# One even product for each pair of rows, and mirror rows stored by index

## The chip, the cores and the metric

The kernel runs on one core of a Trainium2 chip. The time is the device time of one execution, in microseconds (us). It was run three times, and once more under the hardware profiler, on the same kind of core; the profile times each instruction of that execution.

## The reference

The input x has 8 images of 3072 rows and 256 columns. The reference takes a two-dimensional Fourier transform of each image, keeps the real part, and puts the 24576 resulting rows through a small feed-forward layer with three inputs to a maximum:

```python
X = np.fft.fft(np.fft.fft(x, axis=1), axis=2).real
h = np.maximum(np.maximum(x @ w1, x @ w2), x @ w3)   # x: the 24576 rows of X
out = h @ w_out                                      # 256 -> 768 -> 256
```

All of x, the weights (256 x 768 and 768 x 256) and the output are float32.

## The kernel before

**The mathematics.** A row of the transform at sequence position s and its mirror at 3072 - s have the same even part and opposite odd parts, up to a sign in one column. The kernel therefore holds for each image two bf16 tiles, `tE` (even) and `tO` (odd), each 128 by 1536, one column for each pair of rows, and gets from each pair the row and the mirror row. Row 1536 of each image is made apart (`l2_mid`).

The maximum is written as a linear part plus a rest: w1's part goes straight through w_out (folded together in the weight `gw`: columns 0 to 255 for the even part, 256 to 511 for the odd one; `gwr` is the odd half with the sign of the mirror). The rest needs the maximum of 0 and two differences, whose weights are `gE`, `gO` and, for the step from the row to its mirror, `gD`.

**The stages.** For each image:

- Stage 1 (`Mix.s`, L305): 64 small matmuls of 96 columns in 13 pieces, each evicted by ScalarE (ACT) to `ub`.
- Folds (`Mix.fold`, L316): VectorE (DVE) adds and subtracts mirrored parts into `zE` and `zO`.
- Stage 2 (`Mix.k`, L337): six groups of 128-column matmuls, each evicted by ACT into 512 columns of `tE` or `tO`. `Mix.end` (L365) makes the middle row's column and lets GpSimd (POOL) write reversed copies `tEr` and `tOr` (L374, L375).
- Hidden layer: 18 *units* for each image, three blocks of 512 columns by six slices `jc` of 128 hidden features. A unit does four matmuls of 512 columns (L384, L385) into two PSUM banks, `pse2` and `pse3`. ACT then takes the relu of the first (L398), and DVE the maximum with the second (L399) into `hp`. One unit later `finish` adds the two `gD` matmuls (L392) on the same banks, and ACT and DVE make `hm`, the mirror's hidden values, in the same way; the last argument `hm[:, jc, ::-1]` writes them in reversed order.
- Output layer (`l2_block`, L411): for each of four sub-blocks of 128 columns, and for the row and its mirror, eight matmuls of 256 columns into one half of a PSUM bank `po`: even part (L402), odd part (L404), six hidden slices (L407). Then DVE copies `po` to `ot` (L427) and the SyncE queue (SP) issues the stores (L434): two of 128 rows, or, for the sub-block with rows 0 and 12, four shorter ones. A store writes every 24th row of the output, 1 KB each. The reversed copies are what make the mirror's rows come out in that order.

**What sets the order.** The order is written out by hand; each engine works through its own instructions in that order, and waits on semaphores. In each unit the code issues: the four matmuls of this unit and its `hp` operations; `finish` of the unit before; up to 11 matmuls of the output layer of the block before (`l2_some(11)`, a generator that is advanced one matmul at a time); and then what `plan` holds for this unit (L536 to L555): stage-1 pieces, folds and stage-2 groups of the next image, the weight products of the start, the casts of the image after the next (`turn_chunk`, POOL, L117), and the loads (`fetch`, SP). A block has 64 output matmuls and six units, so 66 turns.

PSUM has eight banks: two for `pse2`, two for `pse3`, two for `po`, and two (`ps_f`) that stage 1, stage 2 and the weight products share in turn. `ot` has four buffers.

**Start and end.** x for image 0 comes through POOL's queue (converted on the way) and SP's; stage 1 of image 0 needs all of it. The tables of sines are made meanwhile. At the very end the output layer of the last block runs by itself.

Of the kernel before, what the change touches and what calls it, by code (L numbers as in the profile page):

```python
# [11 lines left out]
INT32 = mybir.dt.int32  # L12
# [21 lines left out]
def kernel(  # L34
# [48 lines left out]
    gE = [consts.tile([128, DFF], BF16, name=f"gE{i}", tag=f"gE{i}") for i in range(2)]  # L83
    gO = [consts.tile([128, DFF], BF16, name=f"gO{i}", tag=f"gO{i}") for i in range(2)]
    gD = [consts.tile([128, DFF], BF16, name=f"gD{i}", tag=f"gD{i}") for i in range(2)]
    gw = consts.tile([128, 512], BF16, tag="gw")
    gwr = consts.tile([128, 256], BF16, tag="gwr")
    sgn = consts.tile([128, 1], FP32, tag="sgn")
    dif = consts.tile([128, 1], FP32, tag="dif")
    t_mid = consts.tile([128, 2, B], BF16, tag="t_mid")  # L90
# [68 lines left out]
    for jh in range(2):  # L159
# [4 lines left out]
        if jh == 0:  # L164
            first_half = wld
    nc.gpsimd.dma_start(out=wout_bf.rearrange("p (jc c) -> p jc c", jc=NJC),
                        in_=moe_w_out.rearrange("(jc p) c -> p jc c", jc=NJC))
    nc.gpsimd.memset(zO.rearrange("p (c r) -> p c r", r=26)[:, :, 24:26], 0.0)
    nc.gpsimd.memset(zO[:, 0:26], 0.0)

# [100 lines left out]
    def prep_second():  # L271

        for jp in range(NJC // 2):
            pst = ps_f.tile([128, 512], FP32, name="pst", tag="ps")
            for k in range(2):
                jc = jp * 2 + k
                for fc in range(2):
                    nc.tensor.matmul(
                        pst[:, k * 256:(k + 1) * 256],
                        w1_bf[:, fc * DFF + jc * 128: fc * DFF + jc * 128 + 128],  # L280
                        md[fc], start=(fc == 0), stop=(fc == 1))
            nc.vector.tensor_copy(out=g1t[:, jp * 512:(jp + 1) * 512], in_=pst)
            yield
        psw = ps_f.tile([128, 512], FP32, name="psw", tag="ps")
        for half in range(2):
            for jc in range(NJC):
                nc.tensor.matmul(
                    psw[:, half * 256:(half + 1) * 256],
                    g1t[:, jc * 256 + half * 128: jc * 256 + half * 128 + 128],
                    wout_bf[:, jc * 256:(jc + 1) * 256],  # L290
                    start=(jc == 0), stop=(jc == NJC - 1))
        nc.vector.tensor_copy(out=gw, in_=psw)
        nc.scalar.activation(out=gwr, in_=psw[:, 256:512], func=AX.Copy, scale=sgn)
        yield

    class Mix:
# [67 lines left out]
        def end(self):  # L364
            er = self.zE.rearrange("p (c r) -> p c r", r=24)  # L365
            orr = zO.rearrange("p (c r) -> p c r", r=26)
            ps3 = ps_f.tile([128, 512], FP32, name="ps3", tag="ps")
            nc.tensor.matmul(ps3[:, 0:1], er[:, :, 0], cos_t[:, 64:65], start=True, stop=True)
            nc.tensor.matmul(ps3[:, 1:2], orr[:, :, 0], nsin_t[:, 64:65], start=True, stop=False)
            nc.tensor.matmul(ps3[:, 1:2], orr[:, :, 24], cos_t[:, 64:65], start=False, stop=True)  # L370
            nc.scalar.copy(out=t_mid[:, :, self.b], in_=ps3[:, 0:2])
            tEr = t_pool.tile([128, NHALF], BF16, name="tEr", tag="tEr")
            tOr = t_pool.tile([128, NHALF], BF16, name="tOr", tag="tOr")
            nc.gpsimd.tensor_copy(tEr, self.tE[:, ::-1])  # L374
            nc.gpsimd.tensor_copy(tOr, self.tO[:, ::-1])  # L375
            self.flipped = tEr, tOr

    def unit_plus(te, to, jc, n):

# [18 lines left out]
        nc.scalar.activation(out=stmp[:, 0:n], in_=pses[0][:, 0:n], func=AX.Relu)  # L398
        nc.vector.tensor_tensor(out=dst, in0=src3, in1=stmp[:, 0:n], op=ALU.max)  # L399

    def l2_half(po, te, to, wo, hcols, n):
        nc.tensor.matmul(po, te, gw[:, 0:256], start=True, stop=False)  # L402
        yield
        nc.tensor.matmul(po, to, wo, start=False, stop=False)  # L404
        yield
        for jc in range(NJC):
            nc.tensor.matmul(po, hcols(jc), wout_bf[:, jc * 256:(jc + 1) * 256],  # L407
                             start=False, stop=(jc == NJC - 1))
            yield

    def l2_block(b, blk, hp, hm, tt):  # L411

        base = b * S
        for sub in range(4):
            slot = blk * 4 + sub
            r = slot + 1
            po = ps_o.tile([128, 512], FP32, name="po", tag="po")
            cp = slice(slot * 128, slot * 128 + 128)
            cm = slice((11 - slot) * 128, (12 - slot) * 128)
            sp = slice(sub * 128, sub * 128 + 128)  # L420
            sm = slice((3 - sub) * 128, (4 - sub) * 128)
            yield from l2_half(po[:, 0:256], tt[0][0][:, cp], tt[0][1][:, cp],
                               gw[:, 256:512], lambda jc: hp[:, jc, sp], 128)
            yield from l2_half(po[:, 256:512], tt[1][0][:, cm], tt[1][1][:, cm],
                               gwr, lambda jc: hm[:, jc, sm], 128)
            ot = out_pool.tile([128, 512], FP32, name="ot", tag="ot")
            nc.vector.tensor_copy(out=ot, in_=po)  # L427
            if r <= 11:
                stores = [(0, 128, base + r, 0), (0, 128, base + 24 - r, 256)]
            else:  # L430
                stores = [(0, 64, base, 0), (64, 128, base + 12, 0),
                          (0, 64, base + 1548, 256), (64, 127, base + 1560, 256)]
            for (p0, p1, row, c) in stores:
                nc.sync.dma_start(out=out[row: row + 24 * (p1 - p0 - 1) + 1: 24, :],  # L434
                                  in_=ot[p0:p1, c:c + 256])

    def l2_mid():

        hmid = h_pool.tile([128, NJC, B], BF16, name="hmid", tag="hmid")
        n = NJC * B  # L440
        psm = ps_f.tile([128, 512], FP32, name="psm", tag="ps")
        for i in range(2):
            for jc in range(NJC):
                js = slice(jc * 128, (jc + 1) * 128)
                cs = slice(i * n + jc * B, i * n + (jc + 1) * B)
                nc.tensor.matmul(psm[:, cs], gE[i][:, js], t_mid[:, 0, :],
                                 start=True, stop=False)
# [10 lines left out]
        yield from l2_half(po[0:B, 0:256], t_mid[:, 0, :], t_mid[:, 1, :], gw[:, 256:512],  # L458
                           lambda jc: hmid[:, jc, :], B)
# [6 lines left out]
    def l2_some(n):  # L466
        while n > 0 and l2_queue:
            try:
# [2 lines left out]
            except StopIteration:  # L471
                l2_queue.pop(0)

    m = Mix(0)
    x0f = x0_first.rearrange("p (bb dl) -> p dl bb", dl=64)
    for k in range(13):
        m.s(k, x0f, pool=ps_s if k % 4 else ps_f)
    m.fold(0, 0)
    m.fold(0, 1)
    m.fold(1, 0)  # L480
# [53 lines left out]
                second.pop(0)  # L534

    for (u, fn) in ((0, prep_some), (0, prep_some), (1, prep_some), (1, prep_some),  # L536
                    (2, lambda: m.k(0, 1)), (2, lambda: m.k(1, 1)),
                    (3, prep_some), (3, lambda: m.k(0, 2)), (4, prep_some),
                    (4, lambda: m.k(1, 2)), (4, m.end), (5, prep_some), (5, prep_some),
                    (0, lambda: turn_chunk(1, 0)), (2, lambda: turn_chunk(1, 1)),  # L540
                    (4, lambda: turn_chunk(1, 2)), (6, lambda: turn_chunk(1, 3))):
        at(0, u, fn)
# [2 lines left out]
    for b in range(B - 1):  # L545
# [3 lines left out]
        if b + 2 < B:  # L549
            folds = begin[b] + 8  # L550
            for ch in range(4):
                at(b, folds + (0, 0, 0, 4)[ch], lambda b=b, ch=ch: turn_chunk(
                    b + 2, ch, mix(b + 1).folded))
                if b + 3 < B:
                    at(b, UNITS + (0, 1, 4, 5)[ch], lambda b=b, ch=ch: fetch(b + 3, ch))  # L555

    for b in range(B):
        mm = mixes[b]
# [3 lines left out]
        def finish(prev):  # L562
            pses, to, jc, hm = prev
            unit_minus(pses, to, jc)
            unit_out(pses, hm[:, jc, ::-1], TOKB)

        for blk in range(3):
            cs = slice(blk * TOKB, (blk + 1) * TOKB)
# [2 lines left out]
            for jc in range(NJC):  # L571
# [2 lines left out]
                if prev is not None:  # L574
                    finish(prev)
                prev = (pses, tO[:, cs], jc, hm)
                l2_some(11)
                if b == B - 1 and blk == 0:
                    if jc == 0:
                        middle = l2_mid()  # L580
# [4 lines left out]
            l2_some(1000)  # L585
            if blk == 2:
                finish(prev)
            l2_queue.append((lambda b, blk, hp, hm, mm: l2_block(
                b, blk, hp, hm, ((mm.tE, mm.tO), mm.flipped)))(b, blk, hp, hm, mm))

    l2_some(1000)

# [28 lines left out]
```

## Time and profile before

| what | us |
| --- | --- |
| median of three runs (451.18 to 453.09) | 452.06 |
| the profiled execution | 451.85 |
| its span, first to last instruction | 450.1 |
| first stage-1 matmul starts | 21.62 |
| last copy of `po` starts | 444.30 |
| one relu (L398), mean | 0.604 |
| one cast of x (L117), mean | 3.80 |
| one reversed copy (L374), mean | 1.48 |
| a stage-1 eviction of 480 columns (L314), mean | 0.569 |

The profile's page gives the busy time of each engine, the chain of work that ended last (followed back from the last instruction, each step to what released it), and groups of instructions with their count, total and mean time and the idle time before them. A matmul's mean time there is longer than the distance between two of them, because they overlap in the array: 256 columns show 273 ns, and start about 0.11 us apart. The distance between starts, read in the timeline, is what one costs when PE is full. The waits view lists which operation waited for which, with the total, the number and the longest. In the timeline a row with "xN" merges N equal instructions that follow each other; its duration is that of all.

### The profile page before, as it was taken

To read this page: it belongs to the slowest core of one execution; us is meant where nothing else is said; L and a number is where in the kernel's file an instruction comes from. 1 tells how busy PE (TensorE), PEld (TensorE's weight loads), DVE (VectorE), ACT (ScalarE), POOL (GpSimd) and SP (SyncE) were. 2 spreads that over 40 slices of the span, in tenths; PEclk is the share of its full clock that TensorE was granted. 3 is DMA by queue.
4 is the path that set the end of the run, shared out by engine and by line. 5 is a ranking of instruction groups with operands and counts; after the bars stand their busy time and mean duration, and the time that the engine had idled before them with its cause. 6 is when DMAs were issued, how large, how long until landed. Compare 5 with 4: busy or idle time off the path is not lost.

```text
span 450.1 us, 9342 instructions
## 1 busy us (share of the span) xinstructions
PE 416.6 (93%) x3365; PEld 294.9 (66%) x3424; DVE 306.5 (68%) x640; ACT 253.0 (56%) x472; POOL 144.1 (32%) x77
## 2 busy tenths in 40 slices
PE   0099899999999999999999999999999999999994
PEld 0075577777777677767676677767776677766674
DVE  7645669666876588566966678576966678567672
ACT  3587466556655665556655665556655665545440
POOL 7505810590059002930078002920087000200000
PEclk9999999999999999999999999999999999999998
DMA  9999999498617992198717982299512212112223
GB/s 113 122 162 127 130 153 153 149 160 149 139 49 140 157 172 81 55 152 169 157 47 128 173 156 98 71 160 166 132 48 71 70 57 84 51 47 73 72 80 107
DMA packets 132862, 51.54 MB, mean 115 GB/s; under 512 B 105936, under 2 KB 132816, under 8 KB 132816
## 3 DMA queue, kind: packets, MB, share of 16 engines
q1 hardware_dynamic: 118384, 47.99, 54.6%
q0 software_dynamic: 12848, 2.57, 8.1%
q10 hardware_dynamic: 1584, 0.39, 0.6%
q8 instruction: 26, 0.43, 0.4%
q14 instruction: 20, 0.16, 0.1%
HBM read 28.31 MB, written 25.17 MB: 119 GB/s over the span
## 4 chain that ended last, share of the span: by engine, by line
PE 91%; DMA 4%; issue 1%; ACT 1%; POOL 1%; DVE 1%; POOLq 0%; ACTq 0%
PE po L407 28%; PE pse L384 16%; PE pse L392 14%; PE pse L385 11%; PE ps L312 6%; PE po L402 5%; PE po L404 5%; DMA x<-in_x_dram 3%; PE ps L359 1%; PE ps L357 1%; PE ps L350 1%; PE psg L259 1%; PE ps L353 1%; DMA w_bf<-in_moe_w_dram 1%; POOL x L99 1%
## 5 line engine op out<-in xcount | busy, mean ns | idle before, releaser
L398 ACT ACTIVATE stmp<-pse 128x512 bf16<-128x512 f32 x288 | 167.1, 604 | 72.3 <-PE pse L385 53.4
L399 DVE TENSOR_TENSOR hp<-pse,stmp 128x512 bf16<-128x512 f32 x144 | 99.5, 691 | 116.3 <-ACT stmp L398 74.7
L117 POOL CAST x<-xs 96x2048 bf16<-96x2048 f32 x28 | 105.7, 3803 | 197.7 <-PE pse L392 180.7
L384 PE MATMUL pse<-tE,gE 128*128 128x512 bf16 x287 | 108.9, 379 | 2.8 <-DVE hm L399 0.2
L399 DVE TENSOR_TENSOR hm<-pse,stmp 128x512 bf16<-128x512 f32 x144 | 98.7, 686 | 8.1 <-ACT stmp L398 7.8
L385 PE MATMUL pse<-tO,gO 128*128 128x512 bf16 x234 | 88.6, 379 | 0.5 <-ACT tO L362 0.5
L407 PE MATMUL po<-wout_bf,hp 128*128 128x256 bf16 x576 | 86.1, 273 | 0.1
L407 PE MATMUL po<-wout_bf,hm 128*128 128x256 bf16 x576 | 86.1, 273 | 0.0
L392 PE MATMUL pse<-tO,gD 128*128 128x512 bf16 x284 | 84.8, 379 | 0.3
L314 ACT CAST ub<-ps 128x480 bf16<-128x480 f32 (+1 forms) x104 | 52.2, 563 | 43.8 <-PE ps L312 43.8
L427 DVE COPY ot<-po 128x512 f32<-128x512 f32 x96 | 65.6, 683 | 3.8 <-PE po L407 3.8
L407 PEld LDWEIGHTS <-hp 128*128 128x128 bf16 x576 | 56.4, 98 | 16.3
L407 PEld LDWEIGHTS <-hm 128*128 128x128 bf16 x576 | 56.4, 98 | 16.3
L312 PE MATMUL ps<-m24blk,x 96*128 96x96 bf16 x512 | 33.0, 216 | 21.6 <-DMA w_bf<-in_moe_w_dram 21.6
L392 PEld LDWEIGHTS <-gD 128*128 128x128 bf16 x288 | 27.9, 98 | 32.1
L312 PEld LDWEIGHTS <-x 96*128 96x128 bf16 x512 | 30.3, 112 | 22.7 <-DVE dif L243 21.6
L384 PEld LDWEIGHTS <-gE 128*128 128x128 bf16 x288 | 28.6, 99 | 19.8 <-issue 1.2
L385 PEld LDWEIGHTS <-gO 128*128 128x128 bf16 x288 | 28.2, 98 | 19.1 <-issue 0.8
L362 ACT CAST tO<-ps 128x512 bf16<-128x512 f32 x24 | 14.1, 586 | 29.1 <-PE ps L359 29.1
L402 PE MATMUL po<-gw,tE 128*128 128x256 bf16 x96 | 26.2, 273 | 0.2
L404 PE MATMUL po<-gw,tO 128*128 128x256 bf16 x96 | 26.2, 273 | 0.0
L402 PE MATMUL po<-gw,tEr 128*128 128x256 bf16 x96 | 26.2, 273 | 0.0
(109 smaller groups left out, 356.5 us busy)
## 6 DMA issues: line engine op xcount, KB each, us to landing
out_dram<-ot SPq DMA_DIRECT2D x176, 128.0 KB
xs<-in_x_dram SPq DMA_DIRECT2D x112, 192.0 KB
out_dram<-ot SPq DMA_DIRECT2D x24, 64.0 KB
w_bf<-in_moe_w_dram POOLq DMA_DIRECT2D x6, 192.0 KB, 4.9
xs<-in_x_dram SPq DMA_DIRECT2D x8, 96.0 KB
x<-in_x_dram POOLq DMA_DIRECT2D x8, 96.0 KB, 11.9
out_dram<-ot SPq DMA_DIRECT2D x8, 63.0 KB
xs<-in_x_dram ACTq DMA_DIRECT2D x4, 96.0 KB
```

Of the source, the lines that this page charges most:

```text
L117: cast = nc.gpsimd.tensor_copy(turned[b][:, :, ch * 32:(ch + 1) * 32], raw.pop((b, ch)).rearrange("p (bb dl) -> p dl bb", dl=64))
L312: nc.tensor.matmul(ps1[:, i * 96:(i + 1) * 96], x0[:, d0 + i, :], m24blk, start=True, stop=True)
L314: evict(out=self.ub[:, d0 * 96:d1 * 96], in_=ps1[:, 0:(d1 - d0) * 96])
L384: nc.tensor.matmul(pse[:, 0:n], gE[i][:, js], te, start=True, stop=False)
L385: nc.tensor.matmul(pse[:, 0:n], gO[i][:, js], to, start=False, stop=True)
L392: nc.tensor.matmul(pse, gD[i][:, js], to, start=False, stop=True, skip_group_check=True)
L398: nc.scalar.activation(out=stmp[:, 0:n], in_=pses[0][:, 0:n], func=AX.Relu)
L399: nc.vector.tensor_tensor(out=dst, in0=src3, in1=stmp[:, 0:n], op=ALU.max)
L402: nc.tensor.matmul(po, te, gw[:, 0:256], start=True, stop=False)
L404: nc.tensor.matmul(po, to, wo, start=False, stop=False)
L407: nc.tensor.matmul(po, hcols(jc), wout_bf[:, jc * 256:(jc + 1) * 256], start=False, stop=(jc == NJC - 1))
L427: nc.vector.tensor_copy(out=ot, in_=po)
```

## The change

The output layer is made differently, and some things at the start and the end are moved:

- The even part's product is the same for a row and its mirror. It is now made once, for two sub-blocks at a time, into a bank of `ps_f` named `pl` (two matmuls of 256 columns). ACT copies it to a float32 tile `even`.
- The odd part's products for row and mirror become one matmul of 512 columns over `gw[:, 256:768]`, in which `gwr` is now the last third.
- The mirror's hidden matmuls come first in a sub-block, then the row's. DVE adds `even` to both halves of `po` while it takes them to `ot`.
- `hm`, `tE` and `tO` are read in direct order. The reversed copies are gone. The mirror rows therefore come in falling order and are stored by an indirect DMA of POOL, which takes the row numbers from a table `rows_m` made at the start.
- A sub-block has 15 turns of the generator (the 512-column matmul counts as two), a block 60, and `l2_some` takes 10 a unit.
- The last block goes through its sub-blocks in the order 2, 3, 0, 1, and its last addition is split in two halves.
- At the start eight matmuls on `cos_t` into a bank that nothing reads go ahead of stage 1, and DVE takes two of image 0's 13 evictions. In image 0 the third group of stage 2 moves from units 3 and 4 to 6 and 7, and the weight products are spread one to a unit. Casts and loads of later images are spread over more units.

```diff
-            tEr = t_pool.tile([128, NHALF], BF16, name="tEr", tag="tEr")
-            tOr = t_pool.tile([128, NHALF], BF16, name="tOr", tag="tOr")
-            nc.gpsimd.tensor_copy(tEr, self.tE[:, ::-1])
-            nc.gpsimd.tensor_copy(tOr, self.tO[:, ::-1])
...
+    def l2_hidden(po, hcols):
         for jc in range(NJC):
             nc.tensor.matmul(po, hcols(jc), wout_bf[:, jc * 256:(jc + 1) * 256],
-                             start=False, stop=(jc == NJC - 1))
+                             start=False, stop=(jc == NJC - 1), skip_group_check=True)
             yield
...
+        last = b == B - 1 and blk == 2
+        order = (2, 3, 0, 1) if last else range(4)
+        for k, sub in enumerate(order):
...
+            if k % 2 == 0:
+                pl = ps_f.tile([128, 512], FP32, name="pl", tag="ps")
+                for i in range(2):
+                    ci = (slot + i) * 128
+                    nc.tensor.matmul(pl[:, i * 256:(i + 1) * 256], te[:, ci:ci + 128],
+                                     gw[:, 0:256], start=True, stop=True)
+                    yield
+                even = out_pool.tile([128, 512], FP32, name="even", tag="even")
+                nc.scalar.copy(out=even, in_=pl)
+            lin = even[:, (k % 2) * 256:(k % 2 + 1) * 256]
...
+            nc.tensor.matmul(po, to[:, cp], gw[:, 256:768], start=True, stop=True)
+            yield
+            yield
+            split = last and k == 3
+            yield from l2_hidden(po[:, 256:512], lambda jc: hm[:, jc, sp])
...
+            yield from l2_hidden(po[:, 0:256], lambda jc: hp[:, jc, sp])
...
-            nc.vector.tensor_copy(out=ot, in_=po)
+                nc.vector.tensor_tensor(
+                    out=ot.rearrange("p (h c) -> p h c", h=2),
+                    in0=po.rearrange("p (h c) -> p h c", h=2),
+                    in1=lin.unsqueeze(1).to_broadcast([128, 2, 256]), op=ALU.add)
+            lo = 1 if r == 12 else 0
+            nc.gpsimd.indirect_dma_start(
+                out, bass.IndirectOffsetOnAxis(
+                    ap=rows_m[0:128 - lo, b * 12 + slot: b * 12 + slot + 1], axis=0),
+                ot[lo:128, 256:512], None)
             if r <= 11:
-                stores = [(0, 128, base + r, 0), (0, 128, base + 24 - r, 256)]
+                stores = [(0, 128, base + r)]
...
+    warm = ps_s.tile([128, 512], FP32, name="warm", tag="ps")
+    for _ in range(8):
+        nc.tensor.matmul(warm, cos_t[:, 1536:1664], cos_t[:, 1152:1664], start=True, stop=True)
...
     for k in range(13):
-        m.s(k, x0f, pool=ps_s if k % 4 else ps_f)
+        m.s(k, x0f, pool=ps_s if k % 4 else ps_f,
+            evict=nc.vector.tensor_copy if k in (1, 3) else nc.scalar.copy)
...
-                    (2, lambda: m.k(0, 1)), (2, lambda: m.k(1, 1)),
-                    (3, prep_some), (3, lambda: m.k(0, 2)), (4, prep_some),
-                    (4, lambda: m.k(1, 2)), (4, m.end), (5, prep_some), (5, prep_some),
+                    (2, lambda: m.k(0, 1)), (2, lambda: m.k(1, 1)), (2, prep_some),
+                    (3, prep_some), (4, prep_some), (5, prep_some),
+                    (6, lambda: m.k(0, 2)), (7, lambda: m.k(1, 2)), (7, m.end),
...
-                at(b, folds + (0, 0, 0, 4)[ch], lambda b=b, ch=ch: turn_chunk(
+                at(b, folds + (0, 2, 4, 6)[ch], lambda b=b, ch=ch: turn_chunk(
...
-                    at(b, UNITS + (0, 1, 4, 5)[ch], lambda b=b, ch=ch: fetch(b + 3, ch))
+                    at(b, UNITS + (0, 1, 2, 4)[ch], lambda b=b, ch=ch: fetch(b + 3, ch))
...
-            unit_out(pses, hm[:, jc, ::-1], TOKB)
+            unit_out(pses, hm[:, jc, :], TOKB)
...
-                l2_some(11)
+                l2_some(10)
```

More of the change, by code (lines that the diff above doesn't have):

```diff
@@ L85 @@
     gD = [consts.tile([128, DFF], BF16, name=f"gD{i}", tag=f"gD{i}") for i in range(2)]
-    gw = consts.tile([128, 512], BF16, tag="gw")
-    gwr = consts.tile([128, 256], BF16, tag="gwr")
+    gw = consts.tile([128, 768], BF16, tag="gw")
+    rows_m = consts.tile([128, 12 * B], INT32, tag="rows_m")
     sgn = consts.tile([128, 1], FP32, tag="sgn")
@@ L167 @@
                         in_=moe_w_out.rearrange("(jc p) c -> p jc c", jc=NJC))
+    rows_f = gen.tile([128, 12 * B], FP32, tag="rows_f")
+    rows_v = rows_f.rearrange("p (b r) -> p b r", r=12)
+    iota(rows_v, [[S, B], [-1, 12]], base=S - 1, cm=-24)
+    iota(rows_v[:, :, 11], [[S, B]], base=S - 24, cm=-24)
+    late = gen.tile([128, 1], FP32, tag="late")
+    nc.gpsimd.tensor_scalar(out=late, in0=pidx, scalar1=63.0, scalar2=float(S // 2 - 12),
+                            op0=ALU.is_ge, op1=ALU.mult)
+    nc.gpsimd.tensor_scalar(out=rows_v[:, :, 11], in0=rows_v[:, :, 11], scalar1=late,
+                            scalar2=None, op0=ALU.add)
+    nc.gpsimd.tensor_copy(rows_m, rows_f)
     nc.gpsimd.memset(zO.rearrange("p (c r) -> p c r", r=26)[:, :, 24:26], 0.0)
@@ L291, in prep_second @@
                     start=(jc == 0), stop=(jc == NJC - 1))
-        nc.vector.tensor_copy(out=gw, in_=psw)
-        nc.scalar.activation(out=gwr, in_=psw[:, 256:512], func=AX.Copy, scale=sgn)
+        nc.vector.tensor_copy(out=gw[:, 0:512], in_=psw)
+        nc.scalar.activation(out=gw[:, 512:768], in_=psw[:, 256:512], func=AX.Copy, scale=sgn)
         yield
@@ L371, in end @@
             nc.scalar.copy(out=t_mid[:, :, self.b], in_=ps3[:, 0:2])
-            tEr = t_pool.tile([128, NHALF], BF16, name="tEr", tag="tEr")
-            tOr = t_pool.tile([128, NHALF], BF16, name="tOr", tag="tOr")
-            nc.gpsimd.tensor_copy(tEr, self.tE[:, ::-1])
-            nc.gpsimd.tensor_copy(tOr, self.tO[:, ::-1])
-            self.flipped = tEr, tOr
     def unit_plus(te, to, jc, n):
@@ L399, in unit_out @@
         nc.vector.tensor_tensor(out=dst, in0=src3, in1=stmp[:, 0:n], op=ALU.max)
[L401 to L405, printed above, removed]
+    def l2_hidden(po, hcols):
         for jc in range(NJC):
             nc.tensor.matmul(po, hcols(jc), wout_bf[:, jc * 256:(jc + 1) * 256],
-                             start=False, stop=(jc == NJC - 1))
+                             start=False, stop=(jc == NJC - 1), skip_group_check=True)
@@ L409, in l2_half, with l2_block @@
             yield
-    def l2_block(b, blk, hp, hm, tt):
+    def l2_block(b, blk, hp, hm, te, to):
         base = b * S
-        for sub in range(4):
+        last = b == B - 1 and blk == 2
+        order = (2, 3, 0, 1) if last else range(4)
+        for k, sub in enumerate(order):
             slot = blk * 4 + sub
             r = slot + 1
-            po = ps_o.tile([128, 512], FP32, name="po", tag="po")
[L418 to L425, printed above, removed]
-            ot = out_pool.tile([128, 512], FP32, name="ot", tag="ot")
-            nc.vector.tensor_copy(out=ot, in_=po)
+            cp = slice(slot * 128, slot * 128 + 128)
+            sp = slice(sub * 128, sub * 128 + 128)
+            if k % 2 == 0:
[8 more added lines that the diff above has]
+            lin = even[:, (k % 2) * 256:(k % 2 + 1) * 256]
+            po = ps_o.tile([128, 512], FP32, name="po", tag="po")
+            ot = out_pool.tile([128, 512], FP32, name="ot", tag="ot")
+            nc.tensor.matmul(po, to[:, cp], gw[:, 256:768], start=True, stop=True)
[3 more added lines that the diff above has]
+            yield from l2_hidden(po[:, 256:512], lambda jc: hm[:, jc, sp])
+            if split:
+                nc.vector.tensor_tensor(out=ot[:, 256:512], in0=po[:, 256:512], in1=lin,
+                                        op=ALU.add)
+            yield from l2_hidden(po[:, 0:256], lambda jc: hp[:, jc, sp])
+            if split:
+                nc.vector.tensor_tensor(out=ot[:, 0:256], in0=po[:, 0:256], in1=lin,
+                                        op=ALU.add)
+            else:
+                nc.vector.tensor_tensor(
[7 more added lines that the diff above has]
+                ot[lo:128, 256:512], None)
@@ L428, in l2_block @@
             if r <= 11:
-                stores = [(0, 128, base + r, 0), (0, 128, base + 24 - r, 256)]
+                stores = [(0, 128, base + r)]
             else:
-                stores = [(0, 64, base, 0), (64, 128, base + 12, 0),
-                          (0, 64, base + 1548, 256), (64, 127, base + 1560, 256)]
-            for (p0, p1, row, c) in stores:
+                stores = [(0, 64, base), (64, 128, base + 12)]
+            for (p0, p1, row) in stores:
                 nc.sync.dma_start(out=out[row: row + 24 * (p1 - p0 - 1) + 1: 24, :],
-                                  in_=ot[p0:p1, c:c + 256])
+                                  in_=ot[p0:p1, 0:256])
@@ L457, in l2_mid @@
             yield
-        yield from l2_half(po[0:B, 0:256], t_mid[:, 0, :], t_mid[:, 1, :], gw[:, 256:512],
-                           lambda jc: hmid[:, jc, :], B)
+        for k in range(2):
+            nc.tensor.matmul(po[0:B, 0:256], t_mid[:, k, :], gw[:, k * 256:(k + 1) * 256],
+                             start=(k == 0), stop=(k == 1))
+            yield
+        yield from l2_hidden(po[0:B, 0:256], lambda jc: hmid[:, jc, :])
         ot = out_pool.tile([128, 512], FP32, name="ot", tag="ot")
@@ L587 @@
                 finish(prev)
-            l2_queue.append((lambda b, blk, hp, hm, mm: l2_block(
-                b, blk, hp, hm, ((mm.tE, mm.tO), mm.flipped)))(b, blk, hp, hm, mm))
+            l2_queue.append(l2_block(b, blk, hp, hm, tE, tO))
     l2_some(1000)
```

## The prediction

> **What bounds the kernel now.** I read the page's busy shares and its chain first, then PE's waits, then the timeline of the unit that opens a block, then the end.
>
> ```profile
> PE 416.6 (93%) x3365; PEld 294.9 (66%) x3424; DVE 306.5 (68%) x640; ACT 253.0 (56%) x472; POOL 144.1 (32%) x77
> ...
> PE 91%; DMA 4%; issue 1%; ACT 1%; POOL 1%; DVE 1%; POOLq 0%; ACTq 0%
> ...
> L427 DVE COPY ot<-po 128x512 f32<-128x512 f32 x96 | 65.6, 683 | 3.8 <-PE po L407 3.8
> ```
>
> The chain is 91% TensorE (PE). Its complete list of waits:
>
> ```profile
> PE ps L312 <- DMA w_bf<-in_moe_w_dram: 21.6, 1, 21.6
> PE psw L287 <- DVE g1t L282: 0.9, 1, 0.9
> PE ps L368 <- ACT tO L362: 0.7, 1, 0.7
> PE ps L357 <- ACT gD L267: 0.5, 1, 0.5
> PE pse L385 <- ACT tO L362: 0.5, 1, 0.5
> PE pse L384 <- DVE hm L399: 0.2, 1, 0.2
> ```
>
> After the first data arrive (21.6 us) PE waits 2.8 us in all, and all of it before 55 us. So PE streams columns from there to its last matmul, and a matmul removed is time removed, unless its neighbours then wait. How near the neighbours are stands in the timeline of a unit that opens a block (unit 6 of image 3, counted from 0; columns: start, duration, engine, line):
>
> ```profile
> 203.46 0.81 PE L384 MATMUL pse<-tE,gE 128*128 128x512 bf16 x2
> ...
> 204.36 1.10 ACT L398 ACTIVATE stmp<-pse 128x512 bf16<-128x512 f32 x2
> ...
> 204.98 0.82 PE L407 MATMUL po<-wout_bf,hp 128*128 128x256 bf16 x6
> 205.00 0.69 DVE L399 TENSOR_TENSOR hp<-pse,stmp 128x512 bf16<-128x512 f32 x1 [1.05 <-ACT stmp L398]
> ...
> 205.61 0.68 DVE L399 TENSOR_TENSOR hm<-pse,stmp 128x512 bf16<-128x512 f32 x1
> ...
> 207.68 0.71 PE L407 MATMUL po<-wout_bf,hm 128*128 128x256 bf16 x5
> ```
>
> The unit starts at 203.46. Its `hm` write, the sixth and last slice of the block before, ends at 205.61 + 0.68 = 206.29, 2.83 us into the unit. Today PE reads that slice only in the next unit, as the last of the five matmuls from 207.68. Nobody waits.
>
> **The change, part by part.** The working goes against the profiled execution, 451.85 us (span 450.1, so 1.75 around it); the median of the runs is 452.06.
>
> *PE columns.* From the timeline, eight 256-column matmuls take 0.87 us (439.73 to 440.60), 0.109 each; 512-column ones start every 0.215 (206.39, 206.61, 206.82). A sub-block was 16 x 0.109 = 1.744. Now it is 0.109 (its half of `pl`), one 512-wide odd product 0.215, twelve hidden ones 1.308: 1.632. Saved 0.112 x 96 = **-10.7 us**.
>
> *The order inside a sub-block.* This is where a wait comes in. Now `pl` (2 matmuls) and the odd product come first, then the six `hm` matmuls, then `hp`. In a block's first unit PE does six 512-wide matmuls (1.29), `pl` (0.22), odd (0.215) and five `hm` (0.545), and reaches the sixth `hm` slice 2.27 us into the unit. That slice is written in this same unit: DVE first writes this unit's `hp`, then the old block's `hm`. In the new order of instructions the load of that slice waits for DVE. Ready at 2.83, plus 0.05 from a DVE end to the PE start behind it (`g1t` ends 49.55 + 0.68 = 50.23, its reader starts 50.28): PE stands 0.6 us, and all behind it in its queue with it. The same difference at each opening unit (`hm` write's end minus unit start, in the timeline of before): unit 6 of images 2 to 6 2.83, unit 12 2.87, hence 5 x (0.61 + 0.65) = 6.3; image 1 2.60 and 2.79: 0.95; image 7 2.60 twice: 0.75; image 0 3.21 and 2.83: 1.6. Unit 0 is free: no minus products stand before it and `hm` is ready at 1.45 to 1.58 against 1.84. In the final drain the slice is ready at 437.73 + 0.69 = 438.42 and PE would arrive at 436.68 + 1.41 = 438.09: 0.4. Sum **+10.0 us**. Bounds: 5 us if the chain of ACT and DVE runs 0.3 us earlier at all 17 places, 15 if it runs 0.3 later.
>
> *ACT.* 48 copies of `pl`, 128x512 to f32; nearest row, the `tE` cast, 586 ns: 28 us on an engine busy 56%. A unit with stage-1 pieces holds two 0.5 casts and two 0.55 relus in 2.9 us, so one copy more fits, and it stands behind the relus that feed `hm`. In the two `pl` units an image that also have pieces, the second piece takes the bank that `pl` leaves: wanted 1.29 + 1.09 + 0.21 = 2.6 us into the unit, copied by about 2.5 (the relus above end 2.0 in, the copy adds 0.55). Not below 0, since it only adds work; 2 us if each of the 16 is 0.12 late; I take +0.3. Without the cover each copy would cost 0.6.
>
> *DVE.* The copy (683 ns) becomes an addition of the same size; L399, of the same shape and also with one PSUM and one SBUF operand, takes 691. Nothing on the path.
>
> *GpSimd.* Sixteen reversals (1.48 us each) go; 96 indexed stores come. No row shows one. Nearest: its plain loads hold POOL 0.68 to 1.00 us; farthest: its longest instruction, the 3.8 us cast. I take 1.0. Then 12 stores and four casts are 12 + 15 = 27 us of some 50 per image, hidden. Queued behind each other are casts and stores, and for a late store waits one of four `ot` buffers, 16 us of sub-blocks: the casts, spread two units apart, hold a store up 4 us each, and the first of an image also waits for the folds of its own unit. Cover gone above (50 - 15) / 12 = 2.9 us. The small index operations stand before the `zO` memsets (end 23.64); the first fold that needs them starts at 25.5, so 1.9 us of cover for about 1. SP loses 104 stores; its fetches move up, but each still follows the cast that frees its buffer by three units or more (casts 13, 15, 17, 19; fetches 18, 19, 20, 22). In image 0 two stand in the cast's own unit, and SP with the stores behind may wait some 4 us, against the same 16.
>
> [...]
>
> *The start.* Eight matmuls on `cos_t` may run from 16.3 (the table's end) to 19.8 (8 x 0.43, at 0.32 for 384 columns, below), before x lands at 21.6, and DVE takes two of 13 evictions of 0.465. In the trace PE is at half rate long after it starts: 64 stage-1 matmuls take 5.84 us, 91 ns each, against 42 ns later (ten from 203.04 to 203.46), and 384-wide ones start every 0.32 at 28.5 and every 0.16 at 35.3. (The clock column shows full speed there; the spacing decides.) If the eight change nothing, PE stays the pace: -0.2. If they bring full rate, ACT's eleven evictions set it and the weight products halve: about -2.2. I take **-0.8**, nearer the first, because nine busy microseconds, from 21.6 to 30.6, were needed before. [...]
>
> *Image 0.* Moving `k(.,2)`, `end` and the weight products takes away the waits at L287, L368 and L384, 0.9 + 0.7 + 0.2. But units 3 and 4 then hold only 1.73 us of PE work, where the bank of two units ago comes free 2.6 us into a unit and is wanted 0.43 into the next: 0.45 more each. **-0.9**, between -2 and +0.5.
>
> *The end.*
>
> ```profile
> 444.30 0.69 DVE L427 COPY ot<-po 128x512 f32<-128x512 f32 x1 [1.05 <-PE po L407]
> 445.02 2.30 SPq L434 DMA_DIRECT2D out_dram<-ot  x4
> ```
>
> After the last copy SP issues four stores in 2.30 us, and the span ends 2.8 later. Now DVE adds half a tile (about 0.4) and SP issues one store (0.5): -2.1. But the last indexed store starts behind its neighbour on POOL: two of 1.0 from 0.9 us before PE's end, and its landing is unseen. **-1.5**, between 0 and -2.1.
>
> Sum: 451.85 - 10.7 + 10.0 + 0.3 - 0.8 - 0.9 - 1.5 = 448.25, so **448.2 us**.
>
> **Rivals.**
> (a) *The wait at the block's opening is not paid*, because `hm` is ready in time. For it: ACT and DVE idle 44% and 32%. Against: the timeline has 0.6 us missing and nothing in the change speeds that chain. 448.2 - 10.0 = 438.2.
> (b) *The small gains fail*: the clock is not released, the end is held by the indexed store, image 0 gains nothing, and the wait eats the columns: 451.85 - 10.7 + 10.0 + 0.3 - 0.2 = 451.2. For it: each of the three rests on an unseen price.
> (c) *Slower: GpSimd becomes the bound.* Place: its queue, where a store waits behind casts and `ot` is not freed, so DVE, then `po`, then PE stop. It decides above 2.9 us a store. At 3.4, between that point and the 3.8 row, an image needs 12 x 3.4 + 15 = 56 us against 50: six more over seven images with casts, about 490. Against: the 0.68 to 1.00 us rows.
> (d) *The columns are not saved*: PE is paced by something else there. The even spacing of 0.109 speaks against it, and 96 products are really gone. 448.2 + 10.7 = 458.9.
>
> **Numbers.** Forecast 0.58 (443 to 449.6, from the bounds of wait, start and end); (a) 0.14; (b) 0.16; (c) 0.08; (d) 0.04. 0.5% (2.3 us) is about what a measurement of this kernel tells from no change. Faster: forecast and (a), 0.72; same: (b), 0.16; slower: (c), (d), 0.12. The range takes in the forecast, (a) and (b): 437.5 to 453, and leaves out (c) and (d).
>
> **What would show it.** Right: PE's waits list an `hm` load or matmul behind DVE's `hm`, some 17 times, 0.4 to 1.0 us each, 10 us in all, at the openings of blocks; units elsewhere 0.11 us shorter; POOL's stores about 1 us. Wrong: no such wait (a), PE waiting for `po` or `pl`, or POOL busy throughout (c).

## The result: 699.0 us, and where the time went

| | us | ratio to before (95% interval) |
| --- | --- | --- |
| before, median of 4 (450.77 to 453.09) | 451.6 | |
| after, median of 4 (694.38 to 704.42) | 699.0 | 1.548 (1.536 to 1.560) |
| forecast | 448.2, range 437.5 to 453.0 | |

The change made the kernel 55% slower. The page of the changed kernel: the busy times, the chain by engine and by line, and two groups (the last columns are the idle time ahead of the group and what ended most of it).

```profile
PE 452.6 (65%) x3184; PEld 288.3 (41%) x3240; DVE 309.9 (44%) x643; ACT 279.6 (40%) x518; POOL 228.5 (33%) x162
...
DMA 36%; PE 28%; POOL 15%; issue 9%; DVE 6%; ACT 3%; SPq 2%; POOLq 0%; DVEq 0%; ACTq 0%
DMA out_dram<-ot,rows_m 19%; DMA out_dram<-ot 14%; POOL x L117 12%; PE po L408 7%; PE pse L389 5%; PE pse L390 4%; PE pse L397 4%; DMA xs<-in_x_dram 3%; POOL out_dram L452 3%; PE ps L322 3%; DVE hm L404 2%; SPq L99 2%; ACT stmp L403 2%; DVE hp L404 1%; PE po L434 1%
...
L452 POOL DMA_INDIRECT out_dram<-ot,rows_m x96 | 107.1, 1116 | 434.2 <-DMA out_dram<-ot 293.8
...
L447 DVE TENSOR_TENSOR ot<-po,even 128x512 f32<-128x512 f32 x95 | 65.3, 688 | 164.5 <-DMA out_dram<-ot 156.3
```

PE had 91% of the chain and has 28%. First now are two stores to the output: the indexed ones (`out_dram<-ot,rows_m`) and the plain ones (`out_dram<-ot`). An indexed store holds POOL for 1.1 us, as forecast; what is new is the 434 us in which POOL stands idle ahead of these stores, most of it until a *plain* store has landed. The waits of the changed kernel, by engine (total, times, longest):

```profile
SPq L461 <- DMA out_dram<-ot,rows_m: 486.3, 91, 12.6
...
POOL out_dram L452 <- DMA out_dram<-ot: 293.8, 50, 13.9
...
DVE ot L447 <- DMA out_dram<-ot: 156.3, 49, 11.8
...
PE ps L322 <- POOL x L117: 85.0, 7, 24.3
PE po L408 <- DVE hm L404: 72.6, 17, 11.8
```

Read from the top: SP's plain store waits for the indexed store before it to land, POOL's indexed store waits for the plain store before it to land, so the two queues take turns. `ot` is freed late, so DVE adds late, and its `hm` behind that addition is late for PE. The casts (L117) stand in POOL's queue behind the blocked stores, so stage 1 is late too.

Why two stores to different rows should wait for each other: a plain store names its rows. An indexed store names the whole output, 24576 rows, since its rows are known only when it runs. The program orders two writes that may touch the same bytes, so each plain store carries a semaphore wait for the indexed store ahead of it, and the other way round (91 and 50 waits above; with two handles, e1 below, neither is left but for 17.5 us at the kernel's end). Three turns in POOL's timeline:

```profile
239.62 0.98 POOL L452 DMA_INDIRECT out_dram<-ot,rows_m  x1 [11.66 <-DMA out_dram<-ot]
244.63 0.96 POOL L452 DMA_INDIRECT out_dram<-ot,rows_m  x1 [4.03 <-DMA out_dram<-ot]
249.62 0.96 POOL L452 DMA_INDIRECT out_dram<-ot,rows_m  x1 [4.03 <-DMA out_dram<-ot]
```

A turn takes 5.0 us even when nothing disturbs it: the store that starts at 239.62 has landed at 242.05, SP issues from 242.10 to 242.47, that store's landing lets POOL go on at 243.87, and the next indexed store starts 0.76 later. Before, an image took 50.5 us, 4.2 for each of its 12 sub-blocks. So the alternation alone is slower than all of PE's work.

### The profile page after: what moved, and what is told of

Same layout as the page of the kernel before. It is cut to its first block, busy times and chain, and to the rows that moved or that the text cites. A ratio compares the mean times of both kernels' runs of the same rounds, so it can differ in the third digit from the quotient of the medians.

```text
span 697.5 us, 9035 instructions
## 1 busy us (share of the span) xinstructions
PE 452.6 (65%) x3184; PEld 288.3 (41%) x3240; DVE 309.9 (44%) x643; ACT 279.6 (40%) x518; POOL 228.5 (33%) x162
## 4 chain that ended last, share of the span: by engine, by line
DMA 36%; PE 28%; POOL 15%; issue 9%; DVE 6%; ACT 3%; SPq 2%; POOLq 0%; DVEq 0%; ACTq 0%
DMA out_dram<-ot,rows_m 19%; DMA out_dram<-ot 14%; POOL x L117 12%; PE po L408 7%; PE pse L389 5%; PE pse L390 4%; PE pse L397 4%; DMA xs<-in_x_dram 3%; POOL out_dram L452 3%; PE ps L322 3%; DVE hm L404 2%; SPq L99 2%; ACT stmp L403 2%; DVE hp L404 1%; PE po L434 1%
## 5 line engine op out<-in xcount | busy, mean ns | idle before, releaser
L452 POOL DMA_INDIRECT out_dram<-ot,rows_m x96 | 107.1, 1116 | 434.2 <-DMA out_dram<-ot 293.8
L408 PE MATMUL po<-wout_bf,hm 128*128 128x256 bf16 x576 | 92.8, 281 | 72.7 <-DVE hm L404 72.6
L447 DVE TENSOR_TENSOR ot<-po,even 128x512 f32<-128x512 f32 x95 | 65.3, 688 | 164.5 <-DMA out_dram<-ot 156.3
L389 PE MATMUL pse<-tE,gE 128*128 128x512 bf16 x279 | 113.0, 405 | 18.9 <-DVE hm L404 16.6
L117 POOL CAST x<-xs 96x2048 bf16<-96x2048 f32 x28 | 103.4, 3694 | 22.7 <-DMA xs<-in_x_dram 22.6
L390 PE MATMUL pse<-tO,gO 128*128 128x512 bf16 x249 | 101.5, 408 | 1.0 <-ACT tO L372 0.5
L397 PE MATMUL pse<-tO,gD 128*128 128x512 bf16 x280 | 91.7, 409 | 0.8 <-DVE hp L404 0.3
L322 PE MATMUL ps<-m24blk,x 96*128 96x96 bf16 x512 | 35.7, 226 | 86.8 <-POOL x L117 85.0
L408 PEld LDWEIGHTS <-hp 128*128 128x128 bf16 x576 | 59.4, 103 | 29.9 <-issue 13.2
L434 PE MATMUL po<-gw,tO 128*128 128x512 bf16 x96 | 39.3, 410 | 9.7 <-DVE ot L447 9.7
L430 ACT COPY even<-pl 128x512 f32<-128x512 f32 x48 | 28.3, 589 | 11.3 <-PE pl L426 11.1
```

What stands on the lines that cost most here:

```text
L117: cast = nc.gpsimd.tensor_copy(turned[b][:, :, ch * 32:(ch + 1) * 32], raw.pop((b, ch)).rearrange("p (bb dl) -> p dl bb", dl=64))
L322: nc.tensor.matmul(ps1[:, i * 96:(i + 1) * 96], x0[:, d0 + i, :], m24blk, start=True, stop=True)
L389: nc.tensor.matmul(pse[:, 0:n], gE[i][:, js], te, start=True, stop=False)
L390: nc.tensor.matmul(pse[:, 0:n], gO[i][:, js], to, start=False, stop=True)
L397: nc.tensor.matmul(pse, gD[i][:, js], to, start=False, stop=True, skip_group_check=True)
L434: nc.tensor.matmul(po, to[:, cp], gw[:, 256:768], start=True, stop=True)
```

## The experiments

Theory "order" is the above: the waits between stores. Its rival "GpSimd" is nearest to the prediction's rival (c): the indexed store is dear in itself. "Rest" says that the new products and additions cost the time. The time of each kernel was compared with the kernel before on the same chip (median 451.5 to 452.0). Each "Measured" gives the median of all executions and, behind it, the ratio to before with its 95% interval; the experiments are named e1 to e12.

### One handle, two, nine

The edit of e1; e2 has nine handles and `views[1 + slot % 8]`:

```diff
+    views = dram_disjoint_views(out, 2)
+    out = views[0]
...
             nc.gpsimd.indirect_dma_start(
-                out, bass.IndirectOffsetOnAxis(
+                views[1], bass.IndirectOffsetOnAxis(
```

> The changed kernel, with the output named by two handles that the program's dependency tracker takes to be disjoint: GpSimd's indexed stores write through the one, all plain stores through the other. Instructions, rows and bytes stay. Theory 'order' (each plain store waits until the indexed store before it has landed, and each indexed store until the plain one before it has): the waits of SP for indexed stores (486 us) and of POOL for plain stores (294 us) vanish. An indexed store still waits for the indexed one before it, so where two stand back to back POOL pays about 1.1 us of issue and 2.4 us of landing for each: 446 to 480 us. Rival 'GpSimd' (the indexed store itself is the cost, by its time on POOL or its slow transfer): 650 to 700 us, as before this edit.

Measured (e1): 541.8 us, ratio 1.198 (1.194 to 1.202). SP's 486 us of waits for indexed stores are gone, but for 17.5 us at the kernel's end, and POOL no longer waits for plain stores. 157 us of the 247 are back, with POOL's work unchanged at 228.7 us: theory "order" holds, and "GpSimd", which asked for 650 or more, falls. The size was missed: I expected at most 480. What is left, in the waits of SP and of POOL:

```profile
SPq L652 <- DMA out_dram<-ot,rows_m: 17.5, 2, 17.3
...
POOL out_dram L455 <- DMA out_dram<-ot,rows_m: 123.4, 32, 9.9
```

An indexed store waits for the indexed store before it, 32 times, for up to 9.9 us, where I had counted 2.4 us a landing.

> As the kernel with two handles, but the indexed stores take turns among eight handles of their own, so that neither does one of them wait for the one before. Theory 'order': 445 to 452 us, and if it is clearly below the kernel with two handles, the wait of an indexed store for the indexed one before had a price too. Rival 'GpSimd': 650 to 700 us.

Measured (e2): 462.5 us (executions from 460.1 to 473.6), 1.023 (1.019 to 1.026). The waits between indexed stores cost nearly 80 us, and without them 95% of the loss is back. But 10 us more than I expected are left. The view of L455 alone says where to look: its first row has the least, median and longest time on POOL in ns, its last the time to landing.

```profile
L455 POOL DMA_INDIRECT out_dram<-ot,rows_m x96: 954/961/2592, 58.9 to 448.7; - x96
...
DMA to landing us min/median/max: 2.4/3.6/11.4
```

The long ones are every twelfth store (counted from 0: 11, 23, 35 and so on, and 93 in the last image), 2.55 us on POOL each, and 10.4 to 11.4 us to landing where that is recorded. They are the ones with 127 rows.

### No indexed store, and only the indexed store

> The changed kernel with its mirror rows stored by SP's plain stores as before the change, in rising order of rows, so the mirror rows land in the reverse order of rows within each store; nothing else of the computation is changed. GpSimd issues no indexed store. Theory 'order', and rival 'GpSimd' too: 446 to 452 us, that is the forecast's 448.2 less what it gave the end (its 1.5). Rival 'rest' (the even part's separate product, the addition by DVE or the new order inside a sub-block cost the time): above 600 us.

```diff
-            nc.gpsimd.indirect_dma_start(
-                out, bass.IndirectOffsetOnAxis(
-                    ap=rows_m[0:128 - lo, b * 12 + slot: b * 12 + slot + 1], axis=0),
-                ot[lo:128, 256:512], None)
...
+                stores = [(0, 128, base + r, 0), (0, 128, base + 24 - r, 256)]
```

Measured (e3): 449.2 us, 0.995 (0.993 to 0.997). The rest of the change is worth 0.5%, where 0.8% was forecast for the whole. "Rest" falls.

> The kernel before the change, with only this added: the mirror rows go out through GpSimd's indexed stores into the whole output, in rising order of rows, so that the output is the same. Products, reversals, copies by DVE and plan of the work are those of before. Theory 'order', and rival 'GpSimd' too: about 7 us for each pair of stores, 96 of them and 21 us ahead of them: 600 to 700 us. Rival 'rest': within 1% of 452 us.

```diff
+            nc.gpsimd.indirect_dma_start(
+                out, bass.IndirectOffsetOnAxis(
+                    ap=rows_m[0:n, b * 12 + slot: b * 12 + slot + 1], axis=0),
+                ot[0:n, 256:512], None)
...
-                stores = [(0, 128, base + r, 0), (0, 128, base + 24 - r, 256)]
+                stores = [(0, 128, base + r, 0)]
```

Measured (e4): 733.8 us, 1.624 (1.620 to 1.628): above the range, and above the changed kernel. This one edit is the whole loss, and the rest of the change takes a little of it back. POOL keeps 16 reversals here, in the same queue, and the casts stand close together: twelve of the steps from one indexed store to the next have three casts, or two reversals and a cast, between them, and take 118 us, where twelve at 5.0 us would be 60.

### The twelfth store

> The kernel with nine handles, with one more edit: the twelfth indexed store of each image writes 128 rows in place of 127. Its first partition holds the mirror of token 0, which is token 0 itself, so it goes to that row, and the plain store leaves that row out. In the kernel with nine handles the 88 stores of 128 rows hold POOL 0.96 us and land 2.4 to 7 us after their start, the 8 of 127 rows hold it 2.55 us and land 10.4 to 11.4 us after. Theory 'rows' (the odd number of rows is what makes them slow; the buffer they hold delays DVE at the second block opening of images 1 to 5, 4.7 us, and the end of the kernel, 6.7 us): 449 to 452 us. Rival 'load' (96 indexed stores, whatever their rows, slow SP's queue and the end): 458 to 463 us, as without this edit.

```diff
-            lo = 1 if r == 12 else 0
...
-                    ap=rows_m[0:128 - lo, b * 12 + slot: b * 12 + slot + 1], axis=0),
-                ot[lo:128, 256:512], None)
+                    ap=rows_m[:, b * 12 + slot: b * 12 + slot + 1], axis=0),
+                ot[:, 256:512], None)
...
-                stores = [(0, 64, base), (64, 128, base + 12)]
+                stores = [(1, 64, base + 24), (64, 128, base + 12)]
```

Measured (e5): 454.1 us, 1.005 (1.003 to 1.007), with this view of the store's line:

```profile
L458 POOL DMA_INDIRECT out_dram<-ot,rows_m x96: 954/959/1132, 57.9 to 443.4; - x96
```

No store is slow any more (the longest landing is 6.9 us), and images 1 to 6 go back to the kernel with plain stores but for 0.7 us in image 1 (table below). "Rows" holds for 8.4 of the 13.3 us between e2 and e3; the expected 449 to 452 was missed by 2 us. Of the 4.9 us that it takes more than e3, 4.3 are at the end of the kernel, which "Point by point" takes up.

> The changed kernel as it is, one handle, with only the twelfth indexed store made to write 128 rows. Theory 'order' with 'rows': the alternation of stores stays, but 8 of its 96 steps lose 8.0 us of landing: about 64 us less, 630 to 645 us. Rival 'load': within 1% of 699 us.

Measured (e6): 640.8 us, 1.419 (1.413 to 1.425), within the expected range. So of the 247 us, 58 were the eight 127-row stores inside the alternation. The trace of the changed kernel has the rest: 95 steps from the start of one indexed store to that of the next, 628.8 us in all. At 5.0 us each they would be 475. The eight behind a 127-row store take 13.3 to 15.1 us, 72 us more in sum. Five others take 13.1 to 14.9 us, 45 us more; in each of these SP issues four loads of x ahead of its plain store. The other 37 us are spread over the rest. The 24 casts of 3.7 us in POOL's queue add next to nothing: behind 128-row stores a step with a cast in it takes 5.00 us in the median, one without 5.02, since the cast runs in the time in which POOL would wait for the plain store.

> The kernel with two handles, with the twelfth indexed store of 128 rows: indexed stores still wait for each other, but none of them is slow. Theory 'rows': most of the 79 us that two handles cost more than nine come from the queue behind the 8 slow landings, and go: 452 to 475 us. Rival 'serial' (the wait of each of the 96 for the one before is the cost): 520 us or more.

Measured (e8): 499.0 us (executions from 492.9 to 505.6), 1.104 (1.098 to 1.111), between the two. From two handles to nine, some 45 us (499.0 to 454.1) are the wait of each indexed store for the one before, and some 34 of the 79 were the slow twelfth; with these executions so far apart the split is good to a few us. Both theories had a part.

> A measurement of the price of an indexed store by its number of rows. The kernel with nine handles and hp first; the twelfth indexed store of images 0 to 7 writes 127, 126, 125, 124, 120, 112, 96 and 64 rows, and the rows beyond that number stay unwritten. Known: 128 rows hold POOL 0.96 us and land in 2.4 us at the least, 127 rows 2.55 us and 10.2 us. If oddness is the cause, 127 and 125 are slow and the even counts as quick as 128; if the count must divide by 16 (the DMA engines), 112, 96 and 64 are quick and the others slow; if any count below 128 is slow, all are.

Measured (e9): the eight stores in POOL's timeline, in the order of 127, 126, 125, 124, 120, 112, 96 and 64 rows (start, duration):

```profile
106.96 2.59 POOL L461 DMA_INDIRECT out_dram<-ot,rows_m  x1 [0.20 <-issue]
154.80 1.00 POOL L461 DMA_INDIRECT out_dram<-ot,rows_m  x1 [1.54 <-DVE ot L456]
203.97 1.19 POOL L461 DMA_INDIRECT out_dram<-ot,rows_m  x1 [1.53 <-DVE ot L456]
253.15 1.33 POOL L461 DMA_INDIRECT out_dram<-ot,rows_m  x1 [1.55 <-DVE ot L456]
302.32 1.00 POOL L461 DMA_INDIRECT out_dram<-ot,rows_m  x1 [1.54 <-DVE ot L456]
351.45 0.94 POOL L461 DMA_INDIRECT out_dram<-ot,rows_m  x1 [1.51 <-DVE ot L456]
402.91 0.91 POOL L461 DMA_INDIRECT out_dram<-ot,rows_m  x1 [2.78 <-DVE ot L456]
435.02 0.91 POOL L461 DMA_INDIRECT out_dram<-ot,rows_m  x1 [0.51 <-DVE ot L456]
```

All three guesses fail: 126 is quick, 125 and 124 lie between, and 124 is dearer than 125. In the order of their time on POOL: 127 rows 2.59, 124 rows 1.33, 125 rows 1.19, 126 and 120 rows 1.00, 112 rows 0.94, 96 and 64 rows 0.91 us, each from one store; 128 rows take 0.96 in the median (e5). What sets this order is not shown. It does not matter whether the 127 rows begin at partition 1 (e2, 2.55 to 2.59 us) or at partition 0 (here).

The DMA packets differ too. In the changed kernel the data of the 127-row store that starts at 307.61 go out in 32 packets one after another, over 5.5 us; the 32 packets of the next store, with 128 rows, overlap each other, up to 18 at once, and are done in 0.5 us.

### The order inside a sub-block

> The kernel with nine handles and the 128-row twelfth store, with the six products of hp ahead of the six of hm in each sub-block but the last. PE's wait for the sixth hm slice in each block's opening unit (0.61 and 0.54 us in images 2 to 6, 0.99 and 0.61 in image 0, 0.38 twice in image 7) should go, as hm is then reached 0.65 us later: 9 us less than the same kernel with hm first, 440 to 443 us. If those waits only reappear elsewhere (for po, pl or pse): no gain, 449 to 452 us.

```diff
-            yield from l2_hidden(po[:, 256:512], lambda jc: hm[:, jc, sp])
+            if not split:
+                yield from l2_hidden(po[:, 0:256], lambda jc: hp[:, jc, sp])
+            yield from l2_hidden(po[:, 256:512], lambda jc: hm[:, jc, sp])
```

Measured (e7): 449.8 us, 0.991 (0.988 to 0.995), not the expected 440 to 443. Nine executions lie between 444.6 and 454.0, and the profiled one took 451.5. In it images 3 to 6 take the 49.17 us that were expected; image 0 takes 57.2 where e5 took 51.8.

> The kernel with nine handles, 128-row stores and hp first once more, as it was, for a second profile of it: in its first profile image 0 took 57.2 us, where the kernels with hm first took 51.8, since the loads of image 1 landed late (POOL's casts waited for them, and PE for the casts, 7.6 us in all). If that is the luck of the loads, image 0 takes 50.5 to 52 us here or varies again; if hp first causes it, it takes 57 us again. All later images 49.2.

Measured (e10, one execution): 450.9 us, image 0 57.06. This is the kernel of e7 unaltered, though its label says "no warm". The third profile with these orders, e9, has 54.7.

> The changed kernel with SP's plain stores for the mirror rows (in the reverse order of rows within each store), and hp ahead of hm in all sub-blocks but the last: the rest of the change without GpSimd's stores and without the wait for the sixth hm slice. The kernel with hm first took 449.2, 1.17 us an image from the openings of blocks, and 0.4 to 1 more in image 0: 439.5 to 441.5 us. If the wait only moves: 449.

Measured (e11): 441.3 us (executions from 439.5 to 448.8), 0.977 (0.974 to 0.980), as expected, image 0 50.6 in a profiled execution of 439.5. The two longest of PE's waits after the eight matmuls on the table:

```profile
PE ps L322 <- DVE dif L253: 2.1, 1, 2.1
PE po L408 <- DVE ot L442: 0.5, 1, 0.5
```

The wait for `hm` is in that list no more, and nothing has come in its place: the others are 0.5 us and less, once each. In e3 it stood there as this:

```profile
PE po L408 <- DVE hm L404: 6.7, 17, 0.8
```

So hp first alone does not hold image 0 up.

> The kernel with nine handles, 128-row stores and hp first, without the eight matmuls on the cosine table that come ahead of the first data. If they do not change TensorE's rate (matmuls are at half rate until about 31 us with them and without), the first load of gE stays within 0.3 us of 33.5 us, and the time within 0.5% of the same kernel with them, 449.8; if they bring it nearer to full rate, the start is 0.8 to 2.2 us later here.

Measured (e12): 446.1 us (executions from 445.4 to 449.1), 0.990 (0.985 to 0.994). The first load of `gE` is at 33.23 us, so the eight matmuls change nothing at the start. The median is 3.7 us below that of e7, which I had not expected, but it does not show that the eight matmuls cost anything: the executions of e7 reach from 444.6 up, and the two intervals overlap. In the profiles image 0 takes 51.9 us here. In e7 and e10 the casts of image 1 end at 62.2 and 62.0, in e12 at 59.0, in e11 at 58.0; PE wants them at about 58. They wait for their loads, and between 32 and 60 us the DMA engines moved 118 and 114 GB/s there against 136 and 133. What makes the loads slower in some executions stays open.

Of the kernels that store every row in its place (e3, e9 and e11 do not), e12 has the lowest median: 1.0% below before, and 36% below the changed kernel. With the spread of e7 it is not shown to be quicker than that one.

## Point by point: where the prediction was right and wrong

Distances between the first `gE` loads of successive images in the profiles, in us, the last column from the last matmul's start to the end of the span:

| kernel | first unit | image 0 | 1 | 2 | 3 to 6, each | 7 | end |
| --- | --- | --- | --- | --- | --- | --- | --- |
| before | 33.39 | 52.22 | 51.55 | 51.34 | 50.51 | 53.43 | 6.1 |
| e3, plain stores | 33.55 | 51.77 | 51.18 | 51.17 | 50.34 | 53.50 | 4.4 |
| e11, plain, hp first | 33.46 | 50.63 | 50.21 | 50.00 | 49.17 | 52.32 | 4.4 |
| e5, nine handles, 128 rows | 33.33 | 51.78 | 51.87 | 51.17 | 50.34 | 53.50 | 8.7 |
| e12, as e5, hp first, no warm matmuls | 33.23 | 51.85 | 51.29 | 50.00 | 49.17 | 52.32 | 8.7 |

**The step that failed** is the one on GpSimd, which the sum took at nothing ("hidden"). Its price for a store was right (forecast 1.0 us, measured 0.96 in the median of the 88 with 128 rows), and so was "hidden" for that price: with nine handles and 128 rows (e5) images 2 to 7 take as long as with plain stores (e3). But the step named only what the stores stand behind in POOL's queue and who waits for a late one, and asked nothing of what the store itself waits for, nor what then waits for the store on SP. The diff shows it: the first operand is `out`, whole. The waits that the change adds there were never in the sum, and they are nearly the whole error: of the 251 us between forecast and result, 236 went when the handles took the waits away (e2). Rival (c) had the place (POOL's queue, then `ot`, DVE, `po`, PE) and put its point at 2.9 us a store; a store with its waits takes 5.0 us in the alternation. Its price, 490, was for a mechanism that is not the one. The cover of four `ot` buffers, "16 us of sub-blocks", was wrong for the same reason: a late store was taken to delay only itself, but a store that waits for the other queue delays every one behind it in both.

A second assumption inside that step, that a store is a store, had a part in this: 58 us inside the alternation (e6), and 8 with nine handles (e5). The twelfth of each image, with 127 rows, was in the diff too.

**PE columns, -10.7:** right to the digit. An image without waits takes 49.17 in place of 50.51 (e11, images 3 to 6), 1.34 less, and 12 x 0.112 is 1.34.

**The wait for the sixth `hm` slice, +10.0:** right, with 9.4 measured. In e3 the waits view has `PE po <- DVE hm` 17 times, as forecast, and PE's matmuls stand apart 0.61 us at unit 6 and 0.54 at unit 12 of images 3 and 5 (forecast 0.61 and 0.65), 0.99 and 0.61 in image 0 (1.6 in sum, forecast 1.6), 0.38 twice in image 7 and 0.38 in the drain (forecast 0.75 and 0.4). Unit 12 of image 3 in e3's timeline:

```profile
221.16 0.71 PE L408 MATMUL po<-wout_bf,hm 128*128 128x256 bf16 x5
...
221.51 0.68 DVE L404 TENSOR_TENSOR hm<-pse,stmp 128x512 bf16<-128x512 f32 x1
...
222.24 0.28 PE L408 MATMUL po<-wout_bf,hm 128*128 128x256 bf16 x1 [0.37 <-DVE hm L404]
```

Five `hm` matmuls start at 221.16, the sixth is due 5 x 0.109 later, at 221.70, and starts at 222.24, when DVE has written its slice (221.51 + 0.68). Putting hp first took 9.1 us from the images: 1.14 + 0.97 + 5 x 1.17 + 1.18. In the changed kernel the same 17 waits have grown to 72.6 us, where DVE itself waits 156.3 us for `ot`.

**ACT's copies, +0.3, and DVE's addition, 0:** the 1.34 us leave no room for either; the addition takes 688 ns.

**The start, -0.8:** nothing. The first unit starts at 33.55 with the eight matmuls (e3), 33.39 before and 33.23 without them (e12). They ran at half rate themselves (0.43 us each, where 512 columns take 0.215 in image 3 of the kernel before), for 3.4 us from 16.3, and 2.6 us after the last of them started the stage-1 matmuls start 89 ns apart, against 88 before. The half rate ends between 28.7 and 30.9 us in the profiles with the eight matmuls, and at 28.9 (e12), 30.5 (before) and 30.7 (e4) without them. So the eight matmuls did not bring the full rate, and the 2.2 us that the prediction gives for that case did not come. The range of the step held no effect at all at its near end (-0.2), and the value leaned the wrong way.

**Image 0, -0.9:** right in size. In image 0's distance lie only two of its three blocks' output layers, 8 sub-blocks, so its share of the saved columns is 8 x 0.112 = 0.9. From before to e11 it loses 1.59, which leaves -0.7 for this step; from before to e3 it loses 0.45, which is 0.9 of columns less 1.6 of waits and 1.15 more.

**The end, -1.5:** behind the last matmul -1.7 with plain stores, but +2.6 with indexed ones (8.7 against 6.1). The same edit, the last addition in two halves, costs 0.7 ahead of it, which the step did not have: PE's last six matmuls, due at 441.28 in e3, wait for the first half's addition.

```profile
441.97 0.82 PE L408 MATMUL po<-wout_bf,hp 128*128 128x256 bf16 x6 [0.51 <-DVE ot L440]
```

So the end is worth -1.0 with plain stores. It also settles image 7 of the table: 16 sub-blocks save 1.8 there, and e11 loses 1.1.

In e5 the last indexed store leaves POOL at 444.36 and has landed at 446.00, SP is through its closing waits at 446.4, and POOL's next instruction comes at 450.93. SP's waits in e5 have it:

```profile
SPq L655 <- PEq L655: 5.2, 2, 4.7
```

The step had bounded this end by 0, "its landing is unseen"; the landing is not what holds it up, and what does is open (last section).

The terms but GpSimd's, with what they measured in e3 (columns, waits, start, image 0, end), are 451.85 - 10.7 + 9.4 + 0.2 - 1.15 - 1.0 = 448.6, and e3's profiled execution took 448.7. The forecast was the time of a kernel with other stores. That its sum comes so near to e3 is in part luck: the start and the end came out 1.5 worse than forecast, and the waits, ACT's copies and image 0 some 1.15 better.

## What to carry to other kernels

When a change brings a new kind of instruction, list the waits it will carry itself, from what it is *said* to read and write, before its duration. Here the indexed store named a whole tensor and was ordered against every other write to it, and one wait for a landing in each direction turned two independent queues into one that alternates. If the rows are known to be disjoint, say so in the program (separate handles; here 699 to 462 us). Measure an indexed store at more than one number of rows (here 128, 112, 96 and 64 rows held POOL for 0.91 to 0.96 us, 124 for 1.33 and 127 for 2.59), and look at the odd one out of a set of stores.

## What the runs showed of the hardware beyond that

- An indexed store of 128 rows of 1 KB holds POOL for 0.96 us and lands 2.4 us after its start at the least (the median too in the changed kernel; 3.6 in e2); with 127 rows it is 2.55 to 2.66 us and 9.9 to 11.4 us in the changed kernel, and up to 2.81 and 12.0 us in e1.
- After its last indexed store POOL went on only 6.57 us after that store's end, alike in six kernels with 128 rows (e5, e6, e7, e8, e10, e12), though in e5 the store had landed after 1.6 us and SP was through 4.6 us before. It was 3.7 us in the changed kernel, where SP was through only 0.2 us before, 3.7 in e1 and 7.9 in e2. What POOL does in that time no view shows.
- In the kernels in which PE waits long, the granted clock was lower: the mean was 0.851 in the changed kernel, 0.845 in e4, 0.863 in e6, 0.919 in e1, against 0.99 in e3. This may add to those times, and no run separates it.
